# Windowed attention feeding a four-expert mixture: moving the masks between engines, reloading the first rows, and giving the last outputs a second home

## The chip, the cores and the metric

One core of a Trainium2 chip runs the kernel. The metric is the device time in microseconds of one execution. Times come from timed runs; the profile is one further execution taken by the hardware profiler.

## The reference

Four batches of eight heads, 768 tokens, head width 64. A token attends to the four first tokens ("sinks") and to the last 128 tokens. The result, as 3072 tokens of 512 features, goes through all four experts, weighted by normalised probabilities.

```python
scores = scale * np.matmul(q, k.transpose(0, 1, 3, 2))
keep = (pos[None, :] < 4) | ((rel >= 0) & (rel < 128))     # rel = query position - key position
a = softmax(np.where(keep, scores, -1e9))
x = (a @ v).transpose(0, 2, 1, 3).reshape(B * S, H * D)    # 3072 x 512
for e in range(E):                                         # E = 4, w1[e] 512x1024, w2[e] 1024x512
    h = np.maximum(x @ w1[e], 0.0)
    out += p[:, e:e + 1] * (h @ w2[e])
```

## The kernel before, in words

The whole kernel is one long list of instructions for five engines, written in an order that a small planner in the source decides. The planner keeps a clock per engine (`t["pe"]`, `t["dve"]` and so on), estimates when each piece of work could start, and picks the next step for TensorE. Work for the other engines is put in a list (`later`) with a due time and is emitted when the planner's clock reaches it. The constants at the top of the kernel (GATE, FORM, TOKEN, CHORES, SHARE_OF and others) are due times and priorities of that planner. On the chip each engine runs its list in order, held only by semaphores; the planner's clock is not a time of the chip.

**Batches and groups.** A batch's 768 tokens are three groups of 256. For each group and each pair of heads, `scores` computes transposed scores on TensorE (line 701, tile sps), ScalarE takes the exponential into the tile aT (line 739), and the part outside the window must be set to zero. `values` multiplies aT with the rows of v (tile vx, line 780), adds the sinks' part (line 773), and VectorE takes the reciprocal of the sum of weights (line 807). The scaled result (onat) is turned into xT.

**Masks.** Group 0 of the first batch gets its mask as a bias product (line 695). Groups 1 and 2 of the first batch are masked by a VectorE product with mask1, head by head (line 748). From the second batch on, group 0 is masked by VectorE with mask0 for two heads at once (line 720, 768 columns), while groups 1 and 2 are masked on GpSimd, two `affine_select` instructions per pair of heads (line 726, 48 in all): with MASKD = 0 the test at line 732 always sends them there. mask1 is a 512-column tile that lives in a scratch area.

**Rows in the first batch.** `load_first` loads group 0 of q and k as runs of two neighbouring tokens. `load_nat` loads the other blocks with GpSimd-issued DMAs that cast to bf16: for each block of 128 tokens one DMA for q and one for k, in runs of one token (64 values). `transposes` turns them on TensorE with four 128x128 products per pair of heads (line 595, tile tr), and one copy puts them into qkT (line 293). Later batches are turned by DMA instead.

**Experts.** The first layer is computed with a seven-product scheme (P1 to P7, `emit_fast`, line 1177, tiles cps) or plainly (line 1094, tile hps); the second layer again with seven products (`emit_product`, line 1346, tiles acc) or plainly (`emit_second`, line 1417). VectorE forms the sums of operands: token sums T (line 1146), sums S of hidden tiles (lines 1292 and 1271), and chains such as line 1227, on which the next first-layer products wait. The gate times the rectified result is line 1211. At P1 of a second-layer group a tile osb is taken for its output; there is one such buffer, so this waits until the previous group's output has been stored. ScalarE copies into it (line 1389), and DMAs issued from SyncE store it (lines 1338 and 1379).

**Filling.** `idle_products` (line 574) puts dummy products on TensorE where the planner sees nothing to do. Line 1185 is a product that only resets the flags of a bank that `emit_fast` takes.

Of the kernel before, what the change touches and what calls it, by code (L numbers as in the profile page):

```python
# [8 lines left out]
AF = mybir.ActivationFunctionType  # L9
ALU = mybir.AluOpType  # L10
AX = mybir.AxisListType
FP32 = mybir.dt.float32
# [4 lines left out]
def kernel(  # L17
# [46 lines left out]
    MIX = 4  # L64
    SHARE_OF = (0.712, 1.203, 0.916)
    LEAD = (1.333, 0.296)
    DUE = 0
    LOW_PRODUCT = 2.835
    LOW_SECOND = 4.042
    HIGH_PRODUCT = 1.325  # L70
    EARLY = 0.072
    GATE = 5662
    GATE0 = 0
    FORM = 11130
    FORM2 = 9856
    TOKEN0 = 1019
    WAIT2 = 11080
    WAIT1 = 5733
    LATE3 = 3
    TOKEN = 20059  # L80
    MARGIN = 812
    FULL = 8
    STEP0 = 0.153
    READY = 48
    WIDE = 2
    OPEN = 1.818
    ONACT = 1
    ONE = 2
    PAIR = 1
    MASKD = 0  # L90
    GROW = 33585
    ONLY2 = 2
    BEHIND = 1333
    CHORES = 3
    OWN = 2
# [11 lines left out]
    WARM = 6600.0  # L107
    FLIP = 398
    LATE = 0
    LATE1 = 12798  # L110
# [134 lines left out]
    def home(b, i):  # L245
        return f"x{NG * (b % 2) + i % NG}"
# [8 lines left out]
    def load_nat(b, tb):  # L255
        both = sb.tile([P, 2, H, D], BF16, name="rows", tag=home(b, tb), bufs=1) if b else sb.tile(
            [P, 2, H, D], BF16, name="qkn", tag="qkn", bufs=NQB)
# [5 lines left out]
        if not b:  # L263
            qkn_free.pop(0)
            qkn_free.append(1e12)
        nat[b, tb] = both
# [181 lines left out]
    nc.sync.dma_start(out=dp, in_=moe_domain_probs.rearrange("(tb p) e -> tb p e", p=P))  # L448
    nc.sync.dma_start(out=pr, in_=moe_domain_probs.rearrange("(p j) e -> p j e", p=P))

# [41 lines left out]
    for h in range(H):  # L492
        r = 32 * (h // 2) + NSINK * (h % 2)
        nc.sync.dma_start(
            out=vsf[r:r + NSINK, :, 0:D], in_=v[:, h, 0:NSINK, :].rearrange("b j d -> j b d"),
        )
    ident = consts.tile([P, P], BF16, name="ident")
    for sgn in (1, -1):
# [27 lines left out]
    LOW = 32768.0  # L526
    low = [lent[:, 5 * P:8 * P], lent[:, 8 * P:12 * P]]
    nc.vector.tensor_scalar(
# [3 lines left out]
    nc.vector.memset(low[0][0:NSINK, 0:2 * P], 0.0)  # L532
    x = low[1].rearrange("p (n c q) -> p n c q", n=2, c=2)
    nc.scalar.activation(out=x[:, :, 0], in_=two, func=AF.Copy, scale=-LOW)
    nc.scalar.activation(out=x[:, :, 1], in_=two, func=AF.Copy, scale=LOW, bias=-LOW)
# [45 lines left out]
    def transposes(b, g, hp):  # L581
# [10 lines left out]
        for i in range(2):  # L592
            for tt in range(2):
                rows = first["qk"[i]][:, tt, hs] if (b, g) == (0, 0) else nat[b, 2 * g + tt][:, i, hs]
                nc.tensor.transpose(trs[i if (b, g) == (0, 0) else 0][:, i, tt], rows, ident)
        done = pe(4 * P, ready, n=4)
        dst = qkT[b][:, :, hp, g * G:(g + 1) * G]
# [84 lines left out]
    def scores(b, hp, g, more=False):  # L682
# [34 lines left out]
        else:  # L717
            def mask_both(at):
                def run(engine):
                    nc.vector.tensor_mul(a, a, m[:, None, :].to_broadcast([P, 2, w]))  # L720
                    masked(dve(2 * w, rate=1.92))
# [15 lines left out]
        for ph in range(2):  # L737
            def run(engine, ph=ph):
# [8 lines left out]
                def mask_one(engine):  # L747
                    nc.vector.tensor_mul(a[:, ph], a[:, ph], m)  # L748
                    part(dve(w, rate=1.92))
# [211 lines left out]
    class Mixture:  # L961
# [368 lines left out]
        def emit_product(self):  # L1330
# [6 lines left out]
            def store(at, c=slice(0, Dout)):  # L1337
                nc.sync.dma_start(out=out[r + P:r + 2 * P, c], in_=out_sb[b, g][:, 1, c])
                sp(at)
# [24 lines left out]
            C11, C12, C21, C22 = o[:, 0, 0:G], o[:, 0, G:], o[:, 1, 0:G], o[:, 1, G:]  # L1364
            acc_free[bank], seeded = 1e12, acc_free[1 - bank]
# [3 lines left out]
            def run(engine):  # L1369
# [6 lines left out]
                elif m == "P3":  # L1376
                    nc.vector.tensor_add(C12, C12, x)
                    acc_free[bank] = at = dve(G)
                    nc.sync.dma_start(out=out[r:r + P, :], in_=o[:, 0])
                    sp(at)  # L1380
# [208 lines left out]
```

## Time and profile before

| | |
|---|---|
| timed runs | 365.05, 362.17, 364.51 us; median 364.51 us |
| the profiled execution's own time | 364.18 us |
| its span in the profile | 362.5 us |
| TensorE (PE) busy | 351.1 us, 97% |
| VectorE (DVE) busy | 302.0 us, 83% |
| ScalarE (ACT) busy | 169.9 us, 47% |
| GpSimd (POOL) busy | 103.6 us, 29% |
| granted TensorE clock | 0.999 of full speed |

The span is the time from the first to the last profiled instruction; about 1.7 us of the execution's own time lie around it. In a row of a group, the numbers after the bar are busy time and mean duration of one instruction in nanoseconds, then the idle time of the engine just before them and what ended it. A matmul's duration is longer than the step to the next one, because they are pipelined; VectorE's durations overlap a little too. An engine that waits for the shared port inside an instruction is shown as busy.

### The profile page before, as it was taken

The page shows a single profiled execution, that of the slowest core. Times are in us where ns is not written, and L with a number is a line of the kernel's source. Part 1 is how long each engine was busy: PE and PEld are TensorE (multiplying, and loading weights), DVE is VectorE, ACT ScalarE, POOL GpSimd, SP SyncE. Part 2 cuts the span into 40 slices and gives each one's busy share as a digit, 9 for nine tenths or more (in the row PEclk, how much of TensorE's full clock was granted, in tenths as well). Part 3 has the DMA queues.
Part 4 walks back from the last instruction along what each step waited for, and adds up shares of the span by engine and source line. Part 5 has one row for each costly group of instructions (what it writes and reads, how often), then busy time and mean ns, then how long its engine had stood idle before and what let it go on. Part 6 is the DMA issues. An engine that isn't in the chain of part 4 may idle for free.

```text
span 362.5 us, 11127 instructions
## 1 busy us (share of the span) xinstructions
PE 351.1 (97%) x4640; PEld 303.3 (84%) x4649; DVE 302.0 (83%) x679; ACT 169.9 (47%) x430; POOL 103.6 (29%) x142
## 2 busy tenths in 40 slices
PE   8999999999999989999999999999999999999995
PEld 4585688766688979998998999899899999999974
DVE  4868989997999878998799599699689999979720
ACT  5864542467360692446655632943855313222110
POOL 8955115211290168041532830200620000000000
PEclk9999999999999999999999999999999999999999
DMA  9999999999791299990449996131122111000011
GB/s 175 174 188 199 212 226 175 137 136 156 199 116 24 73 159 153 169 116 29 78 69 96 172 148 128 51 75 28 42 78 57 27 56 50 28 31 31 1 60 59
DMA packets 119479, 37.87 MB, mean 104 GB/s; under 512 B 101356, under 2 KB 114924, under 8 KB 119428
## 3 DMA queue, kind: packets, MB, share of 16 engines
q0 software_dynamic: 78576, 17.31, 55.3%
q1 hardware_dynamic: 39796, 19.32, 26.5%
q8 instruction: 36, 0.59, 0.6%
q10 hardware_dynamic: 1056, 0.52, 0.5%
q14 instruction: 15, 0.12, 0.1%
HBM read 41.03 MB, written 6.34 MB: 131 GB/s over the span
## 4 chain that ended last, share of the span: by engine, by line
PE 77%; DMA 9%; DVE 6%; ACT 3%; POOL 2%; issue 1%; ACTq 0%; DVEq 0%; POOLq 0%
PE cps L1177 32%; PE acc L1346 31%; DMA w<-in_moe_w_dram 6%; PE acc L1417 5%; PE hps L1094 3%; PE od L780 2%; PE sps L701 2%; DMA vx<-in_v_dram 2%; ACT onat L819 1%; DMA out_dram<-osb 1%; DVE T L1146 1%; PE od L773 1%; DVE S L1292 1%; DVE aT L748 1%; DVE onat L810 1%
## 5 line engine op out<-in xcount | busy, mean ns | idle before, releaser
L1177 PEld LDWEIGHTS <-w 128*128 128x128 bf16 x1408 | 86.7, 98 | 5.0 <-issue 1.8
L1211 DVE SCALAR_TENSOR_TENSOR H<-cps,gates 128x512 bf16<-128x512 f32 x102 | 68.6, 683 | 3.8 <-ACT aT L739 2.3
L1346 PEld LDWEIGHTS <-H 128*128 128x128 bf16 x700 | 64.4, 98 | 7.5 <-issue 1.3
L1346 PE MATMUL acc<-w,H 128*128 128x256 bf16 x420 | 56.2, 273 | 0.0
L1177 PE MATMUL cps<-T,w 128*128 128x128 bf16 x704 | 53.2, 219 | 1.2 <-DVE cps L1227 1.2
L739 ACT ACTIVATE aT<-sps 128x512 bf16<-128x512 f32 (+1 forms) x96 | 46.6, 582 | 14.8 <-PE sps L701 14.7
L1177 PE MATMUL cps<-xT,w 128*128 128x128 bf16 x704 | 52.3, 219 | 0.0
L726 POOL TENSOR_SCALAR_AFFINE_SELECT aT<-aT 128x512 bf16<-128x512 bf16 x48 | 30.8, 686 | 64.2 <-ACT aT L739 23.3
L1220 ACT COPY cps<-cps 128x512 f32<-128x512 f32 x44 | 25.3, 580 | 43.6 <-PE cps L1177 36.0
L1389 ACT COPY osb<-acc 128x256 f32<-128x256 f32 x40 | 15.1, 378 | 61.8 <-PE acc L1346 56.6
L819 ACT ACTIVATE onat<-od,R 128x64 bf16<-128x64 f32 x144 | 33.1, 335 | 23.3 <-DVE R L807 23.2
L1346 PE MATMUL acc<-wf,H 128*128 128x256 bf16 x280 | 37.5, 273 | 0.0
L1227 DVE TENSOR_TENSOR cps<-H,cps 128x512 f32<-128x512 f32 x39 | 26.8, 692 | 12.4 <-PE cps L1177 6.4
L1177 PEld LDWEIGHTS <-qkn 128*128 128x128 bf16 x576 | 34.8, 98 | 2.3 <-issue 1.5
L1346 PEld LDWEIGHTS <-S 128*128 128x128 bf16 x320 | 30.2, 98 | 5.1 <-issue 1.9
L1177 PEld LDWEIGHTS <-vf 128*128 128x128 bf16 x480 | 29.3, 98 | 1.1 <-issue 0.4
L1417 PE MATMUL acc<-w,H 128*128 128x512 bf16 x120 | 28.9, 379 | 0.8 <-DMA w<-in_moe_w_dram 0.3
L322 POOL DMA_DIRECT2D vx<-in_v_dram x24 | 21.4, 908 | 27.1 <-PE od L780 17.0
L1233 ACT COPY H<-cps 128x512 f32<-128x512 f32 x39 | 23.1, 595 | 11.3 <-PE cps L1177 11.1
L1177 PE MATMUL cps<-T,qkn 128*128 128x128 bf16 x384 | 26.5, 219 | 0.7 <-DVE H L1118 0.3
L1242 DVE TENSOR_TENSOR H<-H,cps 128x512 f32<-128x512 f32 x39 | 26.5, 679 | 0.3 <-PE cps L1177 0.3
L259 POOL DMA_DIRECT2D rows<-in_q_dram x18 | 16.0, 888 | 35.0 <-DMA qkT<-rows 20.7
(124 smaller groups left out, 553.8 us busy)
## 6 DMA issues: line engine op xcount, KB each, us to landing
w<-in_moe_w_dram POOLq DMA_DIRECT2D x7, 1024.0 KB, 19.0
out_dram<-osb SPq DMA_DIRECT2D x23, 256.0 KB
gates<-gate_rows SPq DMA_DIRECT2D x40, 128.0 KB
vx<-in_v_dram POOLq DMA_DIRECT2D x24, 128.0 KB, 7.7
rows<-in_q_dram POOLq DMA_DIRECT2D x18, 128.0 KB, 6.0
rows<-in_k_dram POOLq DMA_DIRECT2D x18, 128.0 KB, 6.8
w<-in_moe_w_dram POOLq DMA_DIRECT2D x4, 256.0 KB, 7.2
kraw<-in_k_dram ACTq DMA_DIRECT2D x2, 256.0 KB
```

The source lines that it names most:

```text
L322: nc.gpsimd.dma_start(out=vx[tb][:, :, 0:D], in_=v[b, :, tb * P:(tb + 1) * P, :].rearrange("h p d -> p h d"),)
L726: nc.gpsimd.affine_select(out=x[:, :, :, k], in_=x[:, :, :, k], compare_op=ALU.is_ge, fill=0.0, base=min(sgn, 0), pattern=[[0, 2], [0, 2], ...
L739: nc.scalar.activation(out=a[:, ph], in_=sps[ph][:, 0:w], func=AF.Exp, scale=scale)
L819: nc.scalar.mul(o[:, qi, hp, ph * D:(ph + 1) * D], od[:, qi, ph, 0:D], R[:, qi, ph])
L1177: nc.tensor.matmul(y[:, f], lhsT=A[:, d, f * P:(f + 1) * P], rhs=T[:, d], start=(m in ("P1", "P5") and f == 0 and d == 0), stop=(d == 1), ...
L1211: nc.vector.scalar_tensor_tensor(out=dst, in0=src, scalar=0.0, in1=gate, op0=ALU.max, op1=ALU.mult)
L1220: nc.scalar.copy(out=tiles["Y"], in_=y)
L1227: nc.vector.tensor_add(tiles["V"], c5, tiles["X"])
L1233: nc.scalar.copy(out=c5, in_=y)
L1242: nc.vector.tensor_add(c5, c5, y)
L1346: nc.tensor.matmul(x, lhsT=self.operand(b, g, e, m)[:, f], rhs=forms[e][m][:, f], start=(k == 0 and f == 0 and m in (("P1", "P5", "P2") if ...
L1417: nc.tensor.matmul(op, lhsT=H[:, fb // QF, fb % QF, s], rhs=w2_sb[e][:, fb, :], start=(fb == 0), stop=(fb == NFB - 1),)
```

## The change

1. MASKD becomes very large, so that groups 1 and 2 of the later batches are masked on VectorE. mask1 becomes half as wide (256 columns) with a home of its own, and is read twice or four times through a broadcast. The 48 `affine_select` go; 24 VectorE products of 1024 columns come.
2. For groups 1 and 2 of the first batch, `load_nat` loads 256 tokens of q in one DMA and of k in another, in runs of two tokens: four DMAs in place of eight. A partition now holds two neighbouring tokens, so `transposes` takes 64-column pieces into the two halves of a bank, 64 products in place of 32, and the copy into qkT interleaves even and odd tokens.
3. The first quarter of the first expert's w1 is loaded between the v rows of blocks 2 and 3; the domain probabilities' second load is issued after the eight small loads of the sinks' v rows.
4. In the last batch the outputs of groups 0 and 2 take two tiles that formerly held rows, not the buffer osb.
5. The planner's constants have new values, which changes the order on every engine.

```diff
-    SHARE_OF = (0.712, 1.203, 0.916)
-    LEAD = (1.333, 0.296)
+    SHARE_OF = (0.712, 1.17, 0.907)
+    LEAD = (1.333, 0.307)
...
-    GATE = 5662
-    GATE0 = 0
-    FORM = 11130
-    FORM2 = 9856
-    TOKEN0 = 1019
+    GATE = 4459
+    GATE0 = 1390
+    FORM = 17347
+    FORM2 = 18856
+    TOKEN0 = 0
...
-    MASKD = 0
+    MASKD = 99999999
...
-    CHORES = 3
+    CHORES = 1
...
+        if not b:
+            x = sb.tile([P, H, 2 * D], BF16, name="qkn", tag="qkn", bufs=NQB)
+            nc.gpsimd.dma_start(
+                out=x, in_=(q, k)[tb % 2][b, :, tb // 2 * G:(tb // 2 + 1) * G, :].rearrange("h (p t) d -> p h (t d)", t=2),
+            )
...
-    load_v(0, (2, 3))
-    for i in range(4):
+    load_v(0, (2,))
+    load_w1(0, 4, [0])
+    load_v(0, (3,))
+    for i in range(1, 4):
         load_w1(0, 4, [i])
...
-    mask1 = scratch[:, 10 * P:12 * P].bitcast(BF16)
+    mask1 = consts.tile([P, 2 * P], BF16, name="mask1")
...
-                rows = first["qk"[i]][:, tt, hs] if (b, g) == (0, 0) else nat[b, 2 * g + tt][:, i, hs]
-                nc.tensor.transpose(trs[i if (b, g) == (0, 0) else 0][:, i, tt], rows, ident)
+                if (b, g) == (0, 0):
+                    nc.tensor.transpose(trs[i][:, i, tt], first["qk"[i]][:, tt, hs], ident)
+                    continue
+                for ph in range(2):
+                    nc.tensor.transpose(
+                        trs[0][64 * ph:64 * ph + 64, i, tt], nat[b, 2 * g + i][:, 2 * hp + ph, tt * D:(tt + 1) * D], ident,
+                    )
...
-                copy(engine, dst, trs[0].rearrange("c i t p -> c i (t p)"))
+                copy(engine, dst.rearrange("c i (p t) -> c i p t", t=2), trs[0].rearrange("c i t p -> c i p t"))
...
-                    nc.vector.tensor_mul(a, a, m[:, None, :].to_broadcast([P, 2, w]))
+                    n = 2 if g == 0 else 4
+                    x = a if g == 0 else a.rearrange("p h (n w) -> p (h n) w", n=2)
+                    nc.vector.tensor_mul(x, x, m[:, None, :].to_broadcast([P, n, 2 * w // n]))
...
-                out_sb[b, g] = mo.tile([P, 2, Dout], FP32, name="osb", tag="osb", bufs=1)
+                if b == B - 1 and g % 2 == 0:
+                    out_sb[b, g] = [sb.tile([P, Dout], FP32, name=f"osb{i}", tag=home(b - 1, i), bufs=1) for i in range(2)]
+                else:
+                    half_ = mo.tile([P, 2, Dout], FP32, name="osb", tag="osb", bufs=1)
+                    out_sb[b, g] = [half_[:, i] for i in range(2)]
```

More of the change, by code (lines that the diff above doesn't have):

```diff
@@ L64 @@
     MIX = 4
-    SHARE_OF = (0.712, 1.203, 0.916)
-    LEAD = (1.333, 0.296)
+    SHARE_OF = (0.712, 1.17, 0.907)
+    LEAD = (1.333, 0.307)
     DUE = 0
[L68 to L71, printed above, removed]
-    GATE = 5662
-    GATE0 = 0
-    FORM = 11130
-    FORM2 = 9856
-    TOKEN0 = 1019
-    WAIT2 = 11080
-    WAIT1 = 5733
-    LATE3 = 3
[L80 to L84, printed above, removed]
+    LOW_PRODUCT = 2.643
+    LOW_SECOND = 4.19
+    HIGH_PRODUCT = 0.939
+    EARLY = 0.062
+    GATE = 4459
[3 more added lines that the diff above has]
+    TOKEN0 = 0
+    WAIT2 = 15161
+    WAIT1 = 5608
+    LATE3 = 3
+    TOKEN = 18312
+    MARGIN = 1544
+    FULL = 7
+    STEP0 = 0.165
+    READY = 54
     WIDE = 2
-    OPEN = 1.818
+    OPEN = 1.956
     ONACT = 1
@@ L255, in load_nat @@
     def load_nat(b, tb):
-        both = sb.tile([P, 2, H, D], BF16, name="rows", tag=home(b, tb), bufs=1) if b else sb.tile(
-            [P, 2, H, D], BF16, name="qkn", tag="qkn", bufs=NQB)
+        if not b:
[3 more added lines that the diff above has]
+            )
+            lands(("qk", b, tb), H * P, 2 * D, row_free(b, tb))
+            qkn_free.pop(0)
+            qkn_free.append(1e12)
+            nat[b, tb] = x
+            return
+        both = sb.tile([P, 2, H, D], BF16, name="rows", tag=home(b, tb), bufs=1)
         for i, src in enumerate((q, k)):
@@ L496 @@
         )
+    nc.sync.dma_start(out=pr, in_=moe_domain_probs.rearrange("(p j) e -> p j e", p=P))
     ident = consts.tile([P, P], BF16, name="ident")
@@ L526 @@
     LOW = 32768.0
-    low = [lent[:, 5 * P:8 * P], lent[:, 8 * P:12 * P]]
+    low = [lent[:, 5 * P:8 * P], lent[:, 8 * P:10 * P]]
     nc.vector.tensor_scalar(
@@ L532 @@
     nc.vector.memset(low[0][0:NSINK, 0:2 * P], 0.0)
-    x = low[1].rearrange("p (n c q) -> p n c q", n=2, c=2)
-    nc.scalar.activation(out=x[:, :, 0], in_=two, func=AF.Copy, scale=-LOW)
-    nc.scalar.activation(out=x[:, :, 1], in_=two, func=AF.Copy, scale=LOW, bias=-LOW)
+    nc.scalar.activation(out=low[1][:, 0:P], in_=own, func=AF.Copy, scale=-LOW)
+    nc.scalar.activation(out=low[1][:, P:2 * P], in_=own, func=AF.Copy, scale=LOW, bias=-LOW)
     mask0 = consts.tile([P, 3 * P], BF16, name="mask0")
-    mask1 = scratch[:, 10 * P:12 * P].bitcast(BF16)
+    mask1 = consts.tile([P, 2 * P], BF16, name="mask1")
     made = []
@@ L1337, in store @@
             def store(at, c=slice(0, Dout)):
-                nc.sync.dma_start(out=out[r + P:r + 2 * P, c], in_=out_sb[b, g][:, 1, c])
+                nc.sync.dma_start(out=out[r + P:r + 2 * P, c], in_=out_sb[b, g][1][:, c])
                 sp(at)
@@ L1378, in run @@
                     acc_free[bank] = at = dve(G)
-                    nc.sync.dma_start(out=out[r:r + P, :], in_=o[:, 0])
+                    nc.sync.dma_start(out=out[r:r + P, :], in_=o[0])
                     sp(at)
```

19 lines of the change are left out of this document (8 added, 11 removed).

## The prediction

> **What bounds the kernel now.** I read the head of the page first, then TensorE's own waits, the stages, and last the timeline around each wait.
>
> ```profile
> PE 351.1 (97%) x4640; PEld 303.3 (84%) x4649; DVE 302.0 (83%) x679; ACT 169.9 (47%) x430; POOL 103.6 (29%) x142
> ```
>
> TensorE (PE) is busy 351.1 of 362.5 us. Only the missing 11.4 us, and the work itself, can give time back. At the start PE cannot begin before the zeros exist, and after its last product there is only the final store, so the middle holds about 6 us. The waits of PE alone say which engine ends them (columns: total us, times, longest us):
>
> ```profile
> PE acc L574 <- DVE lent L488: 1.4, 1, 1.4
> PE cps L1177 <- DVE cps L1227: 1.2, 1, 1.2
> PE acc L1346 <- ACT osb L1389: 0.9, 1, 0.9
> PE od L780 <- POOL aT L726: 0.8, 2, 0.6
> PE tx L841 <- DVE onat L810: 0.6, 2, 0.4
> ```
>
> The first line is the start and stays. The next three are what this change can reach. The 1.2 us wait is put down to VectorE (DVE), but the timeline shows what held DVE:
>
> ```profile
> 103.44 4.59 DVE L1146 TENSOR_TENSOR T<-xT 128x256 bf16<-128x256 bf16 x1
> 103.66 4.86 POOL L726 TENSOR_SCALAR_AFFINE_SELECT aT<-aT 128x512 bf16<-128x512 bf16 x8
> 107.95 0.72 DVE L1146 TENSOR_TENSOR T<-xT,T 128x256 bf16<-128x256 bf16 x1
> 108.59 0.68 DVE L1227 TENSOR_TENSOR cps<-H,cps 128x512 f32<-128x512 f32 x1
> 109.33 0.61 PE L1177 MATMUL cps<-T,w 128*128 128x128 bf16 x8 [1.19 <-DVE cps L1227]
> ```
>
> One token sum, usually under 0.3 us, lasts 4.59 us while eight selects run on GpSimd (POOL). Behind it on DVE stands L1227, and PE waits for that. So the masks on POOL cost PE the 1.2 us too, not only the 0.8 us where `values` waits for aT.
>
> The 0.9 us stands near the end, as the chain in order of time shows:
>
> ```profile
> 345.82 3.42 DMA out_dram<-osb
> 349.35 0.38 ACT osb L1389
> 349.77 8.91 PE acc L1346 x80
> ...
> 343.33 0.75 DVE L1292 TENSOR_TENSOR S<-S,qkT 128x512 bf16<-128x512 bf16 x2
> ```
>
> The last group's first copy (L1389) needs the buffer osb, which the previous output's store still reads; P6 stands behind that copy. The last row, from the timeline, is P6's operand, formed well before.
>
> Is DVE near its limit? The stages (columns: window, length, then PE, PEld, DVE, ACT, POOL busy, clock, DMA share, GB/s):
>
> ```profile
> 0.00:20.00 20.00, 17.79 (x180) 11.02 (x181) 13.41 (x56) 14.08 (x31) 18.88 (x32) 1.00 1.62 177
> 20.00:60.00 40.00, 39.15 (x417) 28.84 (x419) 33.71 (x81) 18.02 (x34) 12.54 (x15) 1.00 1.46 203
> 60.00:97.00 37.00, 35.85 (x440) 26.90 (x442) 33.22 (x62) 20.23 (x49) 8.86 (x11) 1.00 1.67 155
> 97.00:135.00 38.00, 35.81 (x509) 31.23 (x508) 34.84 (x73) 21.63 (x65) 18.25 (x26) 1.00 0.82 95
> 135.00:270.00 135.00, 134.76 (x1952) 123.05 (x1950) 115.88 (x262) 72.61 (x200) 45.05 (x60) 1.00 0.78 97
> 270.00:335.00 65.00, 65.00 (x949) 62.23 (x947) 60.44 (x124) 20.36 (x47) 0.00 (x0) 1.00 0.14 40
> ```
>
> From 97 to 270 us DVE is busy 34.84 + 115.88 = 150.7 of 173 us, 87%. From 270 to 335 us it is busy 60.44 of 65 us, 93%, and PE still loses nothing: 93% is bearable where the order has slack.
>
> **Masks to VectorE.** The 48 selects run from 103.7 to 265.2 us (first row below). The order of the changed kernel holds no select of aT and 24 masks of 1024 columns on DVE, so this part does what it says. The trace has no such mask, but a product of the same width and type, and the 768-column mask with a broadcast operand:
>
> ```profile
> L726 POOL TENSOR_SCALAR_AFFINE_SELECT aT<-aT x48: 631/652/880, 103.7 to 265.2; 128x512 bf16<-128x512 bf16 x48
> L360 DVE TENSOR_TENSOR wf<-w 128x1024 bf16<-128x1024 bf16 x4 | 2.7, 684 | 0.0
> L720 DVE TENSOR_TENSOR aT<-aT,mask 128x768 bf16<-128x768 bf16 x12 | 6.5, 550 | 0.4 <-ACT aT L739 0.4
> ```
>
> From 768 to 1024 columns the duration goes from 550 to 684 ns, 0.52 ns a column, so the broadcast costs nothing extra and I take 684 ns: 24 x 0.684 = 16.4 us more for DVE. In return DVE stops waiting inside its instructions:
>
> ```profile
> L1146 DVE TENSOR_TENSOR T<-xT x24: 279/285/4592, 14.9 to 284.1; 128x256 bf16<-128x256 bf16 x24
> L1146 DVE TENSOR_TENSOR T<-xT 128x256 bf16<-128x256 bf16 x24 | 12.6, 526 | 1.5 <-DMA xT<-onat 1.5
> L1146 DVE TENSOR_TENSOR T<-xT,T 128x256 bf16<-128x256 bf16 x24 | 8.3, 347 | 0.5
> L1292 DVE TENSOR_TENSOR H<-H 128x512 bf16<-128x512 bf16 x35 | 15.3, 442 | 0.0
> L1292 DVE TENSOR_TENSOR qkT<-qkT 128x512 bf16<-128x512 bf16 x5 | 2.0, 418 | 0.0
> ```
>
> The median token sum is 285 ns and the means are 526 and 347: 24 x (241 + 62) = 7.3 us. The S sums of L1292 run to 418 ns late in the kernel, where POOL is idle, and to about 442 before: three forms x 35 x 24 ns = 2.5 us. So 9.8 us come back, the net is +6.6 us, and DVE's share from 97 to 270 us becomes 157.3 of 173, 91%: below the 93% that cost nothing. On PE's path this is a gain of 1.2 + 0.8 = **2.0 us**; bounds are 0 (the same 2.0 returns as waits for DVE) and 2.0. The mask now queues on DVE: it waits for both exponentials, and whatever stands behind it waits too. The twelve masks of L720 did this at 0.4 us of DVE idle time in all. Twice as many give 0.8 us of DVE time that PE need not see; I take 0, and the rival below prices the other end.
>
> **Outputs in two homes.** The last group's output no longer waits for that store; the groups before it alternate with osb. Gain **0.9 us**. What P6 needs next, its operand S1, is complete at 343.33 + 0.75 = 344.1 us, so no later wait stands behind the removed one. Bounds 0.9 and 0.9.
>
> **Flag products.** The order has four L1185 where it had six.
>
> ```profile
> 104.86 0.38 PE L1185 MATMUL cps<-w 128*128 128x512 bf16 x1
> 105.08 0.33 PE L1177 MATMUL cps<-xT,w 128*128 128x128 bf16 x3
> ```
>
> The step to the next product is 0.22 us: two of them, **0.4 us** gained. One more filler of 256 columns costs **0.1 us** (half that step).
>
> **First rows in two-token runs.** In the start the loads set the pace. Two windows of the DMA view (packets, MB, share of 16 engines), 3.3 us and 4.1 us long, and the pieces of the chain at that place:
>
> ```profile
> q0 software_dynamic: 3756, 0.48, 274.3%
> q0 software_dynamic: 1462, 0.80, 140.7%
> ...
> 13.35 0.33 PE acc L574 x3
> 13.68 0.45 PE tr L595 x8
> ```
>
> The first window holds one-token rows (128 bytes written each), 0.88 ns a packet; the second w1 quarters (512 bytes), 2.8 ns. A two-token run of 256 bytes lies between: by bytes 1.5 ns. Four DMAs of 1024 packets took 3.6 us; two take 3.1 us, at best (0.40 MB/us of reading as in the second window) 2.7, at worst 5.7. So q and k land 0.5 us earlier (bounds: 0.9 earlier, 2.1 later). POOL issues two DMAs fewer here and two fewer for group 2, which pulls what is queued behind them forward. PE uses 0.33 us of it at once, where three fillers stand before the transposes; I take **0.4 us**. The v rows of block 3 now land one w1 quarter later, 1.4 us, which the earlier rows and issues pay back.
>
> **Transposes.** Eight groups of four products become eight of eight, half as wide. Two neighbours go to different halves of the columns. The trace has no 64-column tile; nearest are the sinks in four column quarters and the scores in two row halves (chain pieces: start, length), against today's transposes:
>
> ```profile
> 30.61 0.89 PE tr L595 x16
> 112.15 0.22 PE sinks L662 x4
> 174.19 0.55 PE sps L701 x12
> L595 PEld LDWEIGHTS <-qkn x48: 95/98/152, 5.9 to 31.2; 128*128 128x128 bf16 x48
> L662 PEld LDWEIGHTS <-ksd x24: 92/92/93, 15.4 to 228.3; 128*32 128x32 bf16 x24
> ```
>
> Today's transposes step 0.056 us for 128 columns. Four sinks of 256 columns, side by side, should then take 0.11 and take 0.22; the scores' 2048 columns in pairs should take 0.45 and take 0.55. So tiles do run side by side, and coming and going costs 0.11 us: eight groups, **+0.9 us**. If the pairs did not overlap, 32 x 0.056 = 1.8 us more; at best nothing. The interleaving copies run on DVE and ScalarE beside the next group's transposes; I take nothing for them, and if one is late it stands in the bound above.
>
> The Trainium skill (TensorEngine Tiling (Array Packing), "Restrictions" under "Tile-to-Partition Mapping") says that column tiling switches fast weight load off. By it the 64 half-width loads would stand serially in front of their products. The sinks' loads, in column tiles, take 92 ns and the full-width ones 98, so the trace shows no such price. By the rule the sum would end as in the last rival.
>
> **The sum.** -2.0 - 0.9 - 0.4 + 0.1 - 0.4 + 0.9 = -2.7 us. The profiled execution's own time is 364.18 us (span 362.5 and 1.7 around it), 0.3 below the median 364.51 of the runs shown: **361.5 us**. With the bounds of the terms this case reaches from 360.1 (transposes free, rows 0.9 us earlier) to 363.7 (pairs one after the other, no gain from the rows); the dearest rows would make that 365.8.
>
> **The rivals.** (a) *The waits return under another name.* DVE at 91% delivers aT or T late, and PE's 2.0 us come back as waits for DVE: 361.5 + 2.0 = 363.5. For it speaks that DVE's queue was what held PE at 109 us; against it that that queue was 4.3 us late only because of POOL.
>
> (b) *Masks hold the first-layer chains: slower.* A mask put ahead of L1227 in DVE's order holds the product behind that by its 0.684 us whenever PE has no other step ready. Each exposed mask costs 0.684: five of 24 give 364.9, slower than before; ten give 368.3, over 1% slower; all 24 give 377.9. It decides from five on. For it: every DVE wait of PE lies on such a short chain, and the smaller CHORES and later FORM change what stands in front. Against it: from 270 to 335 us DVE was busier and PE waited 0.0.
>
> (c) *The early stages tighten too.* Up to 97 us PE is idle 2.2 + 0.85 + 1.15 = 4.2 us, 1.4 of it the start. If loads that come earlier and new due times remove half of the other 2.8: 361.5 - 1.4 = 360.1; with the best bound of the transposes 359.2. Against it: such waits come with any order, and the new one has its own.
>
> (d) *Slow narrow weight loads.* If each of the 64 loads stood serially, 64 x 0.098 = 6.3 us against the 1.8 us (32 x 0.056) of today, 4.5 more, less the 0.9 already counted: 365.1. The 92 ns of the sinks' loads beside products that start together speak against it.
>
> **How the numbers follow.** The sum's case gets 0.43, (a) 0.20, (b) 0.15, of which 0.11 with ten masks or more, (c) 0.19, (d) 0.03. A measurement of this kernel can tell about 1% from no change: 360.9 and 368.2 are the marks. Faster: all of (c) but a little, and some 0.20 of the sum's case, 0.38. Slower: 0.11 from (b), 0.12 with a remainder. Within 1%: 0.50. The range is 358.4 to 366.5: down to (c) with the best bounds, up to seven exposed masks; most of what it leaves out is the rest of (b).
>
> **What would show it.** Right: no selects of aT, 24 masks of L734 near 684 ns, no token sum of L1161 over 0.4 us, no wait of L1361 for osb near the end, PE busy near 351 us in a span near 359.8. Wrong: waits of L1192 for L1242 in number (b), waits of L795 for the mask (a), groups of L605 over 0.4 us each (transposes) or starting after 13.68 us (rows).

## The result, and the profile after

The changed kernel takes 362.56 us (median of 20 runs, 361.13 to 365.35), the one before 364.47 us (median of 20, 362.17 to 365.37). The ratio is 0.9958 with a 95% interval of 0.9939 to 0.9977: 0.8 to 2.2 us less, below the 1% that the prediction counts as a difference. The forecast was a gain of 2.7 us, to 361.5. A second series of both kernels (c_after, below) gave 0.9933 [0.9908, 0.9958].

The head of the page of the kernel after, whose profiled execution has a span of 361.2 us (362.5 before):

```profile
PE 351.9 (97%) x4680; PEld 302.7 (84%) x4680; DVE 308.8 (85%) x704; ACT 169.6 (47%) x429; POOL 68.6 (19%) x90
```

TensorE's idle time fell from 11.4 to 9.3 us (361.2 - 351.9), and its work rose by 0.8 us, so 1.3 us of span remain. VectorE does 6.8 us more, where 6.6 were forecast; GpSimd does 35 us less.

TensorE's own waits after (total us, times, longest us):

```profile
PE acc L581 <- DVE lent L493: 1.4, 1, 1.4
PE acc L1361 <- DVE S L1307: 1.1, 2, 0.6
PE sps L713 <- DVE xT L299: 0.4, 1, 0.4
PE cps L1192 <- DVE cps L1242: 0.3, 1, 0.3
```

All three waits that the change could reach are gone as named: the wait behind the token sum (1.2), the wait for the selects (0.8) and the wait for osb near the end (0.9). But a new one stands second: a second-layer product (L1361) waits 1.1 us for the sum S (L1307), a sum of hidden tiles that VectorE (DVE) forms for it. The stages, in the prediction's windows and columns:

```profile
0.00:20.00 20.00, 17.16 (x191) 10.05 (x192) 13.66 (x53) 13.43 (x30) 17.89 (x31) 1.00 1.43 183
20.00:60.00 40.00, 39.53 (x434) 28.68 (x432) 35.11 (x84) 18.16 (x35) 10.52 (x13) 1.00 1.43 205
60.00:97.00 37.00, 36.95 (x474) 27.43 (x473) 33.51 (x62) 22.91 (x55) 12.12 (x16) 1.00 1.63 155
97.00:135.00 38.00, 36.35 (x524) 32.11 (x521) 33.81 (x83) 21.80 (x63) 12.12 (x14) 1.00 1.40 132
135.00:270.00 135.00, 134.53 (x1925) 122.47 (x1923) 121.77 (x277) 70.65 (x198) 15.93 (x19) 1.00 0.66 86
```

Window less PE's busy time is PE's idle time. Before it was 2.21, 0.85, 1.15, 2.19 and 0.24 us in these five stages; now it is 2.84, 0.47, 0.05, 1.65 and 0.47. A second profile of the same kernel (c_after) has 2.27, 0.61, 0.05, 1.00 and 1.38. The stage up to 97 us became better in both; that the first 20 us became worse shows in one of them only. In the stage where the masks' 2.0 us should have appeared, 0.5 us did (1.2 in c_after), and 0.2 (1.1) of that was given back after 135 us. The DMA share of that stage rose from 0.82 to 1.40.

The wide masks of the kernel after (busy us, mean ns; then DVE's idle time just before them and what ended it), and its token sums (ns: least, median, most; then first and last start):

```profile
L734 DVE TENSOR_TENSOR aT<-aT,mask 128x1024 bf16<-128x1024 bf16 x24 | 16.2, 681 | 4.0 <-ACT aT L753 4.0
L1161 DVE TENSOR_TENSOR T<-xT x24: 274/283/293, 15.8 to 284.6; 128x256 bf16<-128x256 bf16 x24
L1161 DVE TENSOR_TENSOR T<-xT,T x24: 281/283/293, 16.1 to 284.8; 128x256 bf16<-128x256 bf16 x24
```

The wide masks cost what the prediction took (681 ns against 684), and no token sum is stretched any more (293 ns at most, 4592 before). But DVE stands idle for 4.0 us ahead of these 24 masks, where the prediction reckoned with 0.8.

Where the new wait comes from, in the timeline of the kernel after (DVE, PE and SyncE's queue). The last row is from the view of line L1307: the waits in DVE's own queue ahead of these sums (ns: least, median, most; then first and last start):

```profile
96.24 0.52 SPq L1454 DMA_DIRECT2D out_dram<-osb  x1
100.06 0.42 DVE L1307 TENSOR_TENSOR S<-H 128x512 bf16<-128x512 bf16 x1
102.58 0.42 DVE L1307 TENSOR_TENSOR S<-S,H 128x512 bf16<-128x512 bf16 x1 [2.00 <-issue]
103.06 0.61 PE L1361 MATMUL acc<-wf,S 128*128 128x256 bf16 x4 [0.58 <-DVE S L1307]
L1307 DVEq EVENT_SEMAPHORE  x2: 21/1462/2904, 99.5 to 99.6; - x2
```

DVE stands idle for 2.00 us in the middle of its sums. The sum that it could not begin writes S1, and S1 takes the space that the second dense group's output (osb0, line 1426) had. So it may not begin before the last store of that output has landed. That store was issued at 96.24 us; in the trace its landing is signalled from 101.50 to 102.50 us, 6.3 us after the issue. The second wait in DVE's queue, 2904 ns long, ends at 102.53, and the sum starts at 102.58. Before, the same store was issued at 96.06 and had landed at 98.08, after 2.0 us. GpSimd's first row loads of the next batch, in the kernel before (first fence) and after (second):

```profile
97.59 0.87 POOL L259 DMA_DIRECT2D rows<-in_q_dram  x1 [0.39 <-issue]
```

```profile
93.10 0.87 POOL L268 DMA_DIRECT2D rows<-in_q_dram  x1 [0.39 <-ACT sinkA L682]
```

They begin 1.5 us after the store in the kernel before and 3.1 us ahead of it in the kernel after, so that they now run beside it.

The end behaves as forecast: between 347.0 and 349.5 us PE was busy for 1.89 us before and is for all 2.50 now.

### The profile page after: what moved, and what is told of

Read it like the earlier page. It is cut to its first block, busy times and chain, and to the rows that moved or that the text cites. A ratio compares the mean times of both kernels' runs of the same rounds, so it can differ in the third digit from the quotient of the medians.

```text
span 361.2 us, 11129 instructions
## 1 busy us (share of the span) xinstructions
PE 351.9 (97%) x4680; PEld 302.7 (84%) x4680; DVE 308.8 (85%) x704; ACT 169.6 (47%) x429; POOL 68.6 (19%) x90
## 4 chain that ended last, share of the span: by engine, by line
PE 77%; DVE 13%; DMA 5%; issue 2%; ACT 1%; POOL 1%; DVEq 0%; ACTq 0%
PE cps L1192 32%; PE acc L1361 29%; PE acc L1436 6%; DVE H L1226 3%; PE hps L1109 3%; PE od L795 2%; PE sps L713 2%; DMA xT<-onat 2%; DMA vx<-in_v_dram 2%; DVE H L1257 1%; DMA out_dram<-osb 1%; DVE T L1161 1%; DVE S L1307 1%; PE od L788 1%; DVE cps L1242 1%
## 5 line engine op out<-in xcount | busy, mean ns | idle before, releaser
L1192 PEld LDWEIGHTS <-w 128*128 128x128 bf16 x1408 | 87.6, 98 | 4.6 <-issue 1.3
L1361 PEld LDWEIGHTS <-H 128*128 128x128 bf16 x720 | 66.2, 98 | 7.4 <-issue 1.1
L1226 DVE SCALAR_TENSOR_TENSOR H<-cps,gates 128x512 bf16<-128x512 f32 x105 | 70.3, 680 | 1.2 <-issue 0.7
L1361 PE MATMUL acc<-w,H 128*128 128x256 bf16 x432 | 58.5, 273 | 0.1
L1361 PE MATMUL acc<-wf,H 128*128 128x256 bf16 x288 | 38.8, 273 | 0.0
L1242 DVE TENSOR_TENSOR cps<-H,cps 128x512 f32<-128x512 f32 x40 | 27.6, 690 | 9.8 <-PE cps L1192 6.7
L1361 PEld LDWEIGHTS <-S 128*128 128x128 bf16 x320 | 29.7, 98 | 5.6 <-DVE S L1307 1.7
L1436 PE MATMUL acc<-w,H 128*128 128x512 bf16 x128 | 30.3, 379 | 0.0
L1248 ACT COPY H<-cps 128x512 f32<-128x512 f32 x40 | 23.7, 593 | 11.5 <-PE cps L1192 11.4
L734 DVE TENSOR_TENSOR aT<-aT,mask 128x1024 bf16<-128x1024 bf16 (+1 forms) x36 | 22.7, 637 | 4.7 <-ACT aT L753 4.7
```

Source lines behind the costliest of these rows:

```text
L734: nc.vector.tensor_mul(x, x, m[:, None, :].to_broadcast([P, n, 2 * w // n]))
L1192: nc.tensor.matmul(y[:, f], lhsT=A[:, d, f * P:(f + 1) * P], rhs=T[:, d], start=(m in ("P1", "P5") and f == 0 and d == 0), stop=(d == 1), ...
L1226: nc.vector.scalar_tensor_tensor(out=dst, in0=src, scalar=0.0, in1=gate, op0=ALU.max, op1=ALU.mult)
L1242: nc.vector.tensor_add(tiles["V"], c5, tiles["X"])
L1248: nc.scalar.copy(out=c5, in_=y)
L1361: nc.tensor.matmul(x, lhsT=self.operand(b, g, e, m)[:, f], rhs=forms[e][m][:, f], start=(k == 0 and f == 0 and m in (("P1", "P5", "P2") if ...
```

## The experiments

Theory A: the gain is smaller because the removed stall behind the selects comes back as other waits around 95 to 115 us, where VectorE, in order, stands behind something that a DMA delivers. Rival B: the interleaving copies and narrow transposes of the start eat the gain. Rival C: the planner's constants, priced at nothing, decide. First each part was put alone into the kernel before.

**The outputs' second home alone (b_osb).** The order on every engine is the one before.

```diff
-                out_sb[b, g] = mo.tile([P, 2, Dout], FP32, name="osb", tag="osb", bufs=1)
+                if b == B - 1 and g % 2 == 0:
+                    out_sb[b, g] = [sb.tile([P, Dout], FP32, name=f"osb{i}", tag=home(b - 1, i), bufs=1) for i in range(2)]
+                else:
...
```

> The kernel before with the last outputs in two homes alone; the order on every engine is the same as before, instruction for instruction. Theory (the sum's own term): the 0.9 us wait of PE at 348.7 us goes and nothing takes its place, so the time falls by 0.9 to 1.1 us, ratio about 0.997. Rival: the store that was late is the one that ends the kernel, so the end stays where it was: 0.0 us.

Measured: 363.03 us against 363.69, ratio 0.9972 [0.9956, 0.9989]. The other waits stayed as they were:

```profile
PE cps L1177 <- DVE cps L1227: 1.3, 1, 1.3
PE od L780 <- POOL aT L726: 0.8, 2, 0.6
```

So this term is 1.0 us (0.0028 x 364; the interval is 0.4 to 1.6), as the prediction had it (0.9). With the order frozen, this removed wait was a gain of its own length.

**The masks alone (b_dvemask),** with the constants of before, so the planner orders the work anew.

```diff
...
-    MASKD = 0
+    MASKD = 99999999
...
-                    nc.vector.tensor_mul(a, a, m[:, None, :].to_broadcast([P, 2, w]))
+                    n = 2 if g == 0 else 4
+                    x = a if g == 0 else a.rearrange("p h (n w) -> p (h n) w", n=2)
+                    nc.vector.tensor_mul(x, x, m[:, None, :].to_broadcast([P, n, 2 * w // n]))
```

> The kernel before with all masks on VectorE with the half-size mask, everything else as before; the planner puts the order together anew with the old constants. Theory of the sum: PE's 1.2 and 0.8 us of waits go, DVE's load rises by about 6.6 us and costs nothing: 2.0 us less, ratio 0.9945. Rival (a): the same 2.0 us come back as waits of PE for DVE or for what DVE waits for: 0.0 us. Rival (b), masks ahead of the first-layer chains: 1 to 4 us more.

Measured: 365.91 us, ratio 1.0059 [1.0036, 1.0082], so 2.1 us slower (1.3 to 3.0). PE's waits, and then the timeline and a piece of the chain at the longest of them:

```profile
PE cps L1179 <- DVE H L1244: 2.1, 1, 2.1
PE cps L1179 <- DVE H L1120: 1.0, 1, 1.0
```

```profile
106.52 7.90 DMA xT<-onat
114.44 0.29 DVE L1148 TENSOR_TENSOR T<-xT 128x256 bf16<-128x256 bf16 x1 [2.67 <-DMA xT<-onat]
115.71 0.61 PE L1179 MATMUL cps<-T,w 128*128 128x128 bf16 x8 [2.05 <-DVE H L1244]
```

No token sum is stretched any more, but DVE now stands 2.67 us before a token sum, because the DMA that turns onat into xT took 7.90 us. The chain (L1244) queued behind that sum is what PE lacks. The wait has moved from a stalled instruction to a late transfer: theory A. Part of the loss is another thing. The profiled execution (367.42 us) is the slowest of the six, and for 3.4 us after this wait its granted clock was one half (last section); two executions at full clock took 365.4 us, 1.7 more than the kernel before. How much of the 2.1 us the clock has in the others was not separated.

**The first rows alone (b_rows):** two-token loads, 64-column transposes, interleaving copy; otherwise the kernel before.

```diff
...
-                copy(engine, dst, trs[0].rearrange("c i t p -> c i (t p)"))
+                copy(engine, dst.rearrange("c i (p t) -> c i p t", t=2), trs[0].rearrange("c i t p -> c i p t"))
...
```

> The kernel before with two-token rows, half-width transposes and the interleaving copy alone; nearly the same order (the copies into qkT go to other engines in places). Theory of the sum: eight transposed groups cost 0.11 us each more, 0.9, and the earlier rows give 0.4 back: 0.5 us more, ratio 1.001. Rival: the interleaving copy on DVE (682 ns in the trace of after against 425 before) makes the scores late, about 0.25 us at several places: 1.0 to 1.5 us more. Second rival: the shorter DMA queue pulls w2 forward and pays for all of it: 0.5 us less.

Measured: 363.54 us, ratio 0.9991 [0.9971, 1.0011]: nothing that can be told from none. Its waits hold three that the kernel before does not have:

```profile
PE sps L712 <- DVE xT L299: 0.4, 1, 0.4
PE sinks L673 <- DVE qkT L299: 0.3, 1, 0.3
PE sps L712 <- ACT qkT L299: 0.2, 1, 0.2
```

These 0.9 us stand behind the copies of the start (L299), 0.7 of them behind copies on DVE. That the earlier rows pay them back is likely, since the time did not change, but no run shows it apart. All three waits are in the kernel after as well, with 0.4, 0.2 and 0.2 us.

**The constants alone (b_newnums),** masks on GpSimd.

```diff
-    FORM = 11130
+    FORM = 17347
...
-    CHORES = 3
+    CHORES = 1
```

> The kernel before with the planner's new constants alone (masks stay on GpSimd, MASKD = 0). Theory: the constants only fit the new parts, alone they bring nothing: within 1 us of before. Rival (c): they are what removes PE's waits between 60 and 97 us (1.1 us of idle time there in before, 0.05 in after): 1 us less. Third: they were chosen for masks on VectorE and cost more with masks on GpSimd: 1 to 3 us more.

Measured: 375.57 us, ratio 1.0308 [1.0271, 1.0345], 11 us slower. Two of its waits:

```profile
PE cps L1177 <- DVE cps L1227: 2.5, 2, 2.0
PE cps L1177 <- DMA xT<-onat: 2.1, 1, 2.1
```

The wait for L1227 has grown from 1.2 to 2.5 us in all, and PE now waits for a turned onat itself. With the masks on GpSimd the new constants are harmful.

Next, the kernel after with one thing taken out. The first three and c_after have the order of the kernel after; from a_onetoken on the planner orders the work anew.

**osb0 in a home of its own (a_ownosb0).** The store no longer stands before S1.

```diff
-                out_sb[g] = mo.tile([P, 2, Dout], FP32, name="osb0", tag=f"wide{g}" if g < 2 else "osb", bufs=1)
+                out_sb[g] = mo.tile([P, 2, Dout], FP32, name="osb0", tag="wide0" if g < 1 else "osb", bufs=1)
```

> The changed kernel, same order on every engine, but the second dense group's output lives in the buffer osb and not in the tile that later holds S1 (tag wide1). Theory: in the changed kernel DVE waits at 100.5 us for the store of that output (issued at 96.24, landing at about 102.4 beside the row loads that GpSimd issues from 93.1 us on), and PE waits 1.1 us for S behind it; without that wait 1.1 to 1.4 us less than the changed kernel, about 0.9925 of before. Rival: DVE is simply full there (masks, S, T), and what follows is late anyway: less than 0.3 us.

Measured: 362.35 us, ratio 0.9939 [0.9918, 0.9959]. The wait for S is gone, and in DVE's queue the long wait ahead of these sums is gone too:

```profile
L1307 DVEq EVENT_SEMAPHORE  x1: 21/21/21, 99.4 to 99.4; - x1
```

The store itself landed as late as in the kernel after (issued at 96.21 us, landed at 102.68). So it was the landing that held the sum.

**The copy without interleaving (a_plaincopy).**

```diff
-                copy(engine, dst.rearrange("c i (p t) -> c i p t", t=2), trs[0].rearrange("c i t p -> c i p t"))
+                copy(engine, dst, trs[0].rearrange("c i t p -> c i (t p)"))
```

> The changed kernel, same order, with the copy into qkT of the first batch's groups 1 and 2 left contiguous, so that their tokens are not put back in order. Theory: the copy on DVE falls from 682 to about 425 ns and the scores behind it start earlier: PE's waits for qkT near 31.9 and 32.9 us (0.23 each) and near 14.7 and 17.4 us shrink, 0.5 to 0.8 us less than the changed kernel. Rival: PE fills the time anyway and the gain stays in the first 40 us: 0.0 at the end.

Measured: 362.33 us, ratio 0.9934 [0.9908, 0.996]. DVE's copies took 425 ns at most (682 in the kernel after), and of PE's waits for these copies only 0.2 us was left. The result of this variant has the tokens in another order.

**32 full-width transposes in place of 64 (a_widetr).**

```diff
-                for ph in range(2):
-                    nc.tensor.transpose(
-                        trs[0][64 * ph:64 * ph + 64, i, tt], nat[b, 2 * g + i][:, 2 * hp + ph, tt * D:(tt + 1) * D], ident,
-                    )
+                nc.tensor.transpose(trs[0][:, i, tt], nat[b, 2 * g + i][:, 2 * hp + tt], ident)
```

> The changed kernel, same order, with 32 full-width transposes in place of the 64 half-width ones; heads and tokens then lie wrongly in qkT for groups 1 and 2 of the first batch. Theory of the sum: leaving out the change of tile shape gives 0.11 us for each of eight groups, 0.9 us less than the changed kernel. Rival: most of these groups stand beside other waits, so 0.0 to 0.3 us less. Rival (d), slow narrow loads: 3 us or more less.

Measured: 361.88 us, ratio 0.9934 [0.991, 0.9957]. The wait for S was absent in this profile and in that of a_plaincopy too, though neither edit touches it. The three lie on one another, and on c_after below, so rival B is not shown. It is not excluded either: the difference of two such ratios is known to about 1.3 us here, and the 0.5 to 0.9 us that were expected would not be seen in it.

**The kernel after once more (c_after),** as a control for those three.

> The changed kernel itself, unaltered, beside the other runs of this call. Both theories: 0.994 to 0.998 of before. Whether PE's wait for S near 103 us (1.1 us) shows again: if it hangs on when a store meets the row loads, it may be absent here; if DVE is full, it must show.

Measured: 362.48 us against 364.83, ratio 0.9933 [0.9908, 0.9958], so a_ownosb0 gains nothing over it. Its PE waits:

```profile
PE acc L581 <- DVE lent L493: 1.4, 1, 1.4
PE od L795 <- DVE aT L734: 0.9, 2, 0.6
PE acc L1361 <- ACT osb L1408: 0.4, 1, 0.4
PE sps L713 <- DVE qkT L299: 0.4, 1, 0.4
```

The same program, and the wait for S did not show; PE waited for a mask instead. The store that S1 stands behind landed at 99.20 us here, 3.9 us after its issue: GpSimd's row loads had begun 0.6 us ahead of it, and 3.1 us in the first profile. DVE did not stand idle for it. So the cause of the wait for S is shown, by the wait in DVE's queue, by a_ownosb0 without it and by this run with an earlier landing. That it costs the kernel time is not shown: a_ownosb0 and c_after cannot be told apart, to about 1.2 us. The stage around 100 us is a close race between VectorE, which works in order, and several transfers, and which one ends last differed between two executions of one program.

**One-token rows in the kernel after (a_onetoken):** the loads, transposes and copy of before.

```diff
...
-            x = sb.tile([P, H, 2 * D], BF16, name="qkn", tag="qkn", bufs=NQB)
...
+        both = sb.tile([P, 2, H, D], BF16, name="rows", tag=home(b, tb), bufs=1) if b else sb.tile(
+            [P, 2, H, D], BF16, name="qkn", tag="qkn", bufs=NQB)
```

> The changed kernel with one-token rows, full-width transposes and the plain copy as before. Theory: the two-token rows cost more on PE and on DVE than the earlier landing gives: 0.5 to 1.5 us less than the changed kernel, 0.992 to 0.994 of before. Rival: the shorter loads carry the whole early stage (60 to 97 us without waits): 1 us more than the changed kernel.

Measured: 373.13 us, ratio 1.023 [1.0206, 1.0255]: 8 us slower. One PE wait is almost all of it; behind it, the same late transfer:

```profile
PE od L784 <- DVE aT L723: 9.0, 3, 7.9
```

```profile
102.72 8.34 DMA xT<-onat
111.09 0.29 DVE L1150 TENSOR_TENSOR T<-xT 128x256 bf16<-128x256 bf16 x1 [5.10 <-DMA xT<-onat]
```

A mask is the name on PE's wait, but the mask is only queued on DVE behind a token sum that waits 5.10 us for xT. The lateness of that transfer alone does not explain this. In c_after it took as long, and the same sum waited 0.88 us:

```profile
101.79 8.76 DMA xT<-onat
110.58 0.29 DVE L1161 TENSOR_TENSOR T<-xT 128x256 bf16<-128x256 bf16 x1 [0.88 <-DMA xT<-onat]
```

What differs is the order. In c_after DVE has other sums and chains to do from 102.35 to 109.69 us; in a_onetoken this block of token sums stands directly behind the block before it, which ended at 105.70. The edit let the planner order the work anew, so this run shows what a bad place in DVE's order costs, and not what the two-token rows are worth.

**The old constants in the kernel after (a_oldnums),** masks on VectorE; the reverse of the constants' diff.

```diff
-    FORM = 17347
+    FORM = 11130
...
-    CHORES = 1
+    CHORES = 3
```

> All parts of the change with the planner's old constants (masks on VectorE). Theory: parts that move loads and masks need their own constants, because the token sums on DVE wait in order for a DMA transpose of onat whose landing the planner only guesses; with the old constants such a wait of 2 us or more shows between 95 and 120 us, as in the kernel before with masks on VectorE alone, and the time is 1 to 4 us above before. Rival: the constants matter only for masks on GpSimd, and this one is within 1 us of the changed kernel.

Measured: 364.31 us, ratio 0.9991 [0.9974, 1.0007], against 0.9933 for c_after beside it: the constants are worth 0.0058 x 364.8 = 2.1 us here (1.0 to 3.2). The wait that they take away:

```profile
PE cps L1192 <- DVE H L1257: 1.6, 1, 1.6
```

DVE stood 2.17 us before a token sum there, as the theory said, but the time is not above that of the kernel before; the rival, within 1 us of the kernel after, did not come true either.

**The masks back on GpSimd in the kernel after (a_pool).**

```diff
-    MASKD = 99999999
+    MASKD = 0
```

> The changed kernel with the masks of the later batches back on GpSimd (MASKD = 0), all else as in the changed kernel. Theory of the sum: PE's waits behind the selects return, 2 us more than the changed kernel, 1.000 of before. Rival: the constants without masks on VectorE misplace the early stage as in the kernel before with the new constants, where 97 to 140 us lost most of its 11 us: 4 us more or worse.

Measured: 369.91 us, ratio 1.0142 [1.0121, 1.0162], 7.4 us slower than c_after (0.0209 x 364.8 = 7.6 by the ratios): the rival's 4 us or more, and not the theory's 2. Its waits are spread over many lines; two of them, and the token sums, of which one is stretched again:

```profile
PE acc L1361 <- DVE H L1226: 1.6, 1, 1.6
PE cps L1192 <- DVE T L1161: 1.3, 1, 1.3
L1161 DVE TENSOR_TENSOR T<-xT x24: 258/283/3028, 14.7 to 291.4; 128x256 bf16<-128x256 bf16 x24
```

**An attempt at a better version (a_best):** the separate home for osb0, the copies of the start's last group on ScalarE, and one constant back.

```diff
...
-    TOKEN0 = 0
+    TOKEN0 = 1019
...
-            later("any", done, 300, run)
+            later("act" if g == 2 else "any", done, 300, run)
```

> The changed kernel with the second dense output in osb (no wait of DVE for its store), the interleaving copies of group 2 all on ScalarE, and the first token sums a little later on DVE (TOKEN0 1019). Theory: the wait near 103 us goes (1.1 us) and the copies near 31 to 33 us no longer hold the scores (0.3 to 0.5): 1.0 to 1.8 us less than the changed kernel in this call, below 0.993 of before. Rival: PE fills such gaps from its other steps and the end moves by less than 0.3 us.

Measured: 364.06 us, ratio 0.9979 [0.9965, 0.9993]: slower than the kernel after beside it, and a miss. Its longest wait behind the start:

```profile
PE cps L1192 <- DVE cps L1242: 1.0, 2, 0.8
```

The wait for S that it aimed at is not there (as in c_after), and others came: two of the three edits change the order on DVE and ScalarE. Which of them did it was not separated. No version measured here can be told to be faster than the kernel after.

## Why the prediction was right or wrong

**Direction and size.** Forecast: a gain of 2.7 us, within 1%. Measured: 0.8 to 2.2 us in one series, 1.5 to 3.4 in the other (0.9908 to 0.9958 of 364.83). The direction and the range held. The size of the first series, 362.56 us, lies midway between the sum's 361.5 and rival (a)'s 363.5; the ratio of the second would give 361.7. The sum came out near partly by luck, and the step that failed is the masks' term together with the constants, which the prediction put at nothing. By stage, the first profile against the one before: PE's idle time fell by 0.85 us up to 97 us (by 1.28 in c_after; about 0.2 of it is lost records, below), for which the sum had no term; by 0.3 us from 97 to 270 us (0.05 in c_after), where the masks' 2.0 were expected; and by some 0.9 us at the end, as forecast. PE's work rose by 0.8 us (+0.6 forecast). The early stages stood in for a part of the masks.

**Outputs in two homes, -0.9: right.** b_osb measured -1.0 alone, in an unchanged order, and nothing stood behind the removed wait.

**Masks, -2.0: price right, term wrong.** The mask's price and the end of the stretched token sums came as worked out. DVE's busy share from 97 to 270 us is (33.81 + 121.77) / 173 = 90%, for 91% forecast. VectorE's net load, +6.8 for +6.6, is near partly by luck: the masks alone brought +5.5 (307.5 us in b_dvemask, 302.0 before), and 1.8 us of the 6.8 are the interleaving copies (below), four in 2.6 us where two plain ones took 0.8. The mistake was to read the two removed waits as the gain. Alone, the masks made the kernel 2.1 us slower, because the same queue on DVE next stands before a DMA (2.67 us in b_dvemask). In the kernel after, PE's idle time in the two stages from 97 to 270 us fell by 0.3 us, not 2.0. Rival (a), the waits back under another name, is what the profiles show in part: 1.1 us for S in the first, and in c_after 0.9 us for two masks. The argument "0.8 us of DVE time that PE need not see" failed in size too: DVE idled 4.0 us ahead of its wide masks. Rival (b) named as its place the wait of the first-layer product for L1227 (L1242 after). That wait is 0.3 us, so (b) did not happen; b_dvemask was slower by another path, a token sum that waits for a DMA and holds the chain behind it. In the profile of a_widetr PE waits 1.0 us in the same way: a token sum stood 2.04 us before a late transfer, with no mask ahead of it.

**The constants, no term: wrong.** They are worth 2.1 us with the masks on VectorE (a_oldnums against c_after), and cost 11 us with the masks on GpSimd (b_newnums). So the parts do not simply add up; what a part is worth depends on the order that the constants make of it.

**Rows -0.4 and transposes +0.9: the parts off.** b_rows gave 0.9991, an interval of 1.1 us less to 0.4 us more, for +0.5 forecast. The rows came earlier than worked out: both two-token loads had landed at 12.10 us, where the last of four landed at 13.58 before, 1.5 us and not 0.5, beyond the bound of 0.9 that the term had. The first transpose of these groups began at 13.0 us (13.5 before; 12.7 in c_after); the products of a group run in pairs:

```profile
12.76 0.57 PE tr L605 x16
13.54 0.36 PE tr L605 x8
```

These are pieces of the chain of c_after: 0.28 us a group where two follow each other and 0.36 alone, against 0.22 before. Coming and going costs 0.06 to 0.14 us a group, around the 0.11 taken. What was wrong was to put the interleaving copies at nothing:

```profile
L299 DVE COPY qkT<-tr x4: 675/682/684, 15.2 to 33.2; 128x512 bf16<-128x512 bf16 x4
L299 ACT COPY qkT<-tr x4: 585/588/592, 13.5 to 32.2; 128x512 bf16<-128x512 bf16 x4
```

On VectorE the copy now takes 682 ns, where the two contiguous copies of that size that DVE made before took 420 on average, and those of a_plaincopy 425 at most; on ScalarE it costs nothing (592 before). PE sees it, with 0.7 of the 0.9 us of waits in b_rows.

**Flag products -0.4 and filler +0.1.** The order has two flag products fewer and one filler more, as forecast; no run put these terms alone.

**Rival (c), early stages tighten: partly true.** Idle time from 60 to 97 us fell from 1.15 to 0.05 us in both profiles, while the first 20 us lost 0.63 in the first and 0.06 in c_after. Not all of the 1.15 was idle:

```profile
81.79 1.90 PE L1417 MATMUL acc<-w,H 128*128 128x512 bf16 x7 [0.32 <-DMA w<-in_moe_w_dram]
84.52 1.89 PE L1417 MATMUL acc<-w,H 128*128 128x512 bf16 x8
```

In the timeline of the kernel before, four such passes in that stage show seven of eight products, while all the weight loads are there. Each missing record leaves a hole of about 0.05 us, 0.2 us together. The 0.32 us ahead of the pass at 81.79 is not such a hole: that pass lasts as long as one with eight products, so its missing product lies inside it. So some 0.9 us of (c) is real.

**Rival (d), slow narrow weight loads: no.** The 64-column loads take 110 ns (98 at full width):

```profile
L605 PEld LDWEIGHTS <-qkn x64: 106/110/111, 13.0 to 32.9; 128*64 128x64 bf16 x64
```

Eight of them one after the other would be 0.88 us a group, and a group takes 0.28 to 0.36. So the serial price, which the prediction itself had derived, is not in this trace. The Trainium skill (TensorEngine Tiling (Array Packing), "Restrictions") states only that column tiling disables fast weight load, and no price. Whether that is the 12 ns no run shows: the sinks' loads, also in column tiles, took 92 ns.

**What stays open.** Which wait ends last between 95 and 115 us in a typical run of the kernel after, and whether the wait for S costs the kernel any time; whether the masks alone would give their 2.0 us in an order written down by hand, which was not tried; what the new places of the first w1 quarter and of the probabilities' load bring, which were never put alone; what share of b_dvemask's 2.1 us is the clock's; and what made a_best slower.

## What to carry to other kernels

Removing a stall from an engine that works in order gives its length only if nothing else on that queue is almost as late, so look up the next late transfer before counting the gain. Where a planner orders the work, its constants are a part of the change with a price of their own, and a part is only worth a number in an order that stays put: freeze the order to measure it. Before building on a small wait in one profile, take a second profile of the same program, and count whether the records around the wait are complete. A row in which a chain passes through a transfer ends where the chain leaves it; the transfer's own landing is what the wait behind it shows.

## What the runs showed of the hardware

Transfers that meet GpSimd's row loads of the next batch are late. A DMA that turns onat into xT took 7.90 us in b_dvemask, 8.34 in a_onetoken and 8.76 in c_after there, and 3.06 us in a quiet stretch of c_after. The output store that S1 stands behind took 2.0 us in the five profiles in which the row loads began after it. Where they began 0.5 to 0.8 us ahead of it (four profiles) it took 3.6 to 4.0 us, 2.1 to 2.4 us ahead (two) 5.5 to 5.8, and 3.1 to 3.6 us ahead (three) 6.3 to 6.5. A load's time in a quiet stretch says little of its time there.

A DVE instruction of 0.28 us was held for 4.59 us in the kernel before (103.44 to 108.03 us) while eight selects ran on GpSimd (103.66 to 108.52). It did not get its turn between two of them. With the selects back on GpSimd in the kernel after (a_pool) such a sum takes up to 3.03 us again.

The granted clock fell in the run with a PE wait of 7.9 us (a_onetoken). Stretches in and after that wait, in the columns of the stages above:

```profile
108.00:111.00 3.00, 0.00 (x0) 0.00 (x0) 0.00 (x0) 0.00 (x0) 0.00 (x0) 0.62 1.58 168
113.00:115.00 2.00, 2.00 (x24) 1.73 (x22) 1.07 (x3) 0.19 (x1) 0.00 (x0) 0.50 0.00 0
115.00:117.00 2.00, 2.00 (x33) 1.86 (x31) 0.94 (x3) 2.00 (x10) 0.00 (x0) 0.86 0.02 4
```

PE's last product before the wait ended at 104.87 us. If the clock goes from full to half in one step, the mean of 0.62 from 108 to 111 us puts that step near 108.7, 3.9 us later. PE goes on at 112.77 us, and its clock is 0.50 up to 115 us and 0.86 on average in the next two, so half speed ends near 115.6 (0.56 us at half and 1.44 at full give 0.86). 2.8 us of work at half speed lose 1.4 us: this stall cost more than its own length. The Trainium skill (TensorE: Matmul & The Clock Gate, "Part 1: The HAM clock gate") names half clock after an idle window of about 3.4 us, and full clock after about 3.4 us of sustained work. The trace agrees on the two clocks, with 3.9 us of idle time ahead of the fall; the way back took 2.8 us of work here, less than the page's figure.

In b_dvemask the clock was halved too, after a wait of only 2.05 us that ended at 115.71 us. What set it off no run separates:

```profile
117.04:120.45 3.41, 3.32 (x32) 2.32 (x30) 3.41 (x8) 2.27 (x8) 0.00 (x0) 0.50 0.09 28
```
